# Loads held until the crossbar transposes of the batch ahead have landed, and a planner told shorter times for these, in an attention and gated-FFN kernel on one core

## The chip, the cores and the metric

The kernel runs on one core of a Trainium2 chip. The metric is the device time of one execution in microseconds (us). Medians of the kernel before lie between 450.0 and 451.1 us from one session to another; single executions lie between 448.9 and 453.2.

Engine names in the profile: PE is TensorE (matmuls), DVE is VectorE, ACT is ScalarE, POOL is GpSimd, SP is SyncE, and "SPq" marks SP's issuing of a DMA.

## The reference

```python
batch, n_heads, seq, head_dim = (8, 12, 448, 64)
scores = scale * q @ k.T                       # per batch and head
attn   = np.maximum(scores, 0.0) ** 2 / S
x      = (attn @ v) -> (B*S, H*D) = (3584, 768)
out    = (np.maximum(x @ w_gate, 0) * (x @ w_val)) @ w_out    # d_ff 1536
```

q, k and v come in float32 as (8, 12, 448, 64), the output is float32. The kernel computes in bfloat16.

## The kernel before

The eight batches run through attention and FFN. TensorE's program interleaves score products of one batch with FFN products of the batch before it, so that TensorE has FFN work while DVE and ACT work on the scores. A score product needs q and k with the head dimension on the partitions, so both have to be transposed. For batches 0 and 1 TensorE does this; for batches 2 to 7 it is done as follows:

1. GpSimd loads k and q of one batch into a tile qk (672 KB each as they land; there are two such tiles), and v into vv. All loads are issued from GpSimd's one in-order queue.
2. DVE copies qk in seven pieces into the tile `spare`, of which there is one.
3. SP issues two DMA transposes through the crossbar, q's half and k's half, from `spare` into qkT. SP also issues the stores of the output, in program order.

```python
def transpose_batch(b):
    ...
    def emit_pair(s, t):                       # step 2, seven DVE copies
        if s == 0:
            box["p"] = spare()[...]
        nc.vector.tensor_copy(box["p"][:, :, s], st.qk[:, :, t, :]...)
    ...
    def emit_x(i):                             # step 3
        nc.sync.dma_start_transpose(out=columns_of(b)[:, i]..., in_=box["p"][64 * i:64 * i + 64]...)
    xo = []
    for i in range(2):
        op = Op({"SP": 0.3}, lambda i=i: emit_x(i), deps=perm + xo[:1], alloc=[st.tbuf] if i == 0 else [],
                reads=[pair], xfer=9.0 if b > 2 else 6.0)
...
for b in range(2, B):                          # GpSimd's order of loads
    load_heads(b, 0, H, "k")                   # k and q
    if b > 3:
        load_heads(b - 1, 0, H, "v")
    if b == 2:
        load_heads(b, 0, H, "v")
    if b >= XBAR_FROM:
        transpose_batch(b)
```

The order of instructions on each engine is decided at build time by a small planner. It walks through all operations with a cost for each (`{"SP": 0.3}` is 0.3 us of SP, `xfer` the time of a transfer) and always starts what can start first. Its numbers never reach the chip. They only set the order of instructions; what waits for what is then settled by semaphores. For SP the end of an operation is its start plus its cost plus 2.0 plus `xfer`. The planner of the kernel before thus takes 0.3 + 2.0 + 6.0 us for a transpose of batch 2, and the second begins after the first (`xo[:1]`).

## Time and profile before

| | before |
|---|---|
| median of 3 runs | 450.43 us (449.41 to 451.0) |
| span of the profiled run | 449.1 us |
| TensorE busy | 428.7 us, 95% |
| TensorE's wait for qkT | 9.9 us, once |

The busy picture of the page has the span in 40 slices of 11.2 us. A digit is the busy share in tenths; PEclk is the clock granted to TensorE, in tenths of full speed; GB/s is what the DMA engines moved.

```profile
PE   6799999937999999999999999999999999999996
PEclk8899999996999999999999999999999999999999
DMA  8999999992693990579146800872002300030014
GB/s 111 198 198 199 202 205 221 197 200 33 80 201 83 166 165 13 93 115 199 18 61 106 168 1 2 123 122 55 1 0 71 74 0 1 1 83 23 1 35 105
```

TensorE is full from the third slice on, except in the ninth and tenth (90 to 112 us), and in the tenth its clock is low too. The DMA engines are full up to that hole, at about 200 GB/s. The list of TensorE's waits names the cause (columns: who waited for whom, us in total, times, longest):

```profile
PE s_ps L468 <- DMA qkT<-spare: 9.9, 1, 9.9
```

The timeline around the hole, in lines of SP, POOL and TensorE (columns: start, us, engine, line, operation, and in brackets the idle time before it with what ended it):

```profile
62.59 0.75 POOL L246 DMA_DIRECT2D qk<-in_k_dram  x1 [5.92 <-PE t_ps L346]
...
75.14 0.75 POOL L246 DMA_DIRECT2D qk<-in_k_dram  x1 [11.06 <-DVE spare L377]
...
75.84 11.20 SPq L387 DMA_TRANSPOSE qkT<-spare  x1
...
81.69 1.49 POOL L246 DMA_DIRECT2D vv<-in_v_dram  x2 [5.07 <-PE s_ps L530]
...
88.53 12.00 SPq L387 DMA_TRANSPOSE qkT<-spare  x1
...
104.22 1.30 PE L468 MATMUL s_ps<-qkT 64*128 64x448 bf16 x6 [9.94 <-DMA qkT<-spare]
...
105.46 2.42 PE L577 MATMUL v_ps<-xT,wv_102 128*128 128x448 bf16 x6
```

The two transposes of batch 2 take 11.2 and 12.0 us to be issued and land 20.9 and 15.6 us after their issue began, while the loads of q and k of batches 3 and 4 and of v of batch 3 run. TensorE stops until they have landed. The windows view shows that the hole costs again after its end (columns: window, length, busy us of PE, PEld, DVE, ACT, POOL, then granted clock, DMA share, GB/s):

```profile
94.30:104.20 9.90, 0.00 (x0) 0.00 (x0) 0.00 (x0) 0.54 (x1) 0.00 (x0) 0.76 1.20 179
104.20:110.00 5.80, 5.78 (x19) 2.17 (x20) 4.30 (x7) 1.35 (x2) 0.00 (x0) 0.52 0.00 0
110.00:112.00 2.00, 2.00 (x15) 0.77 (x13) 0.75 (x2) 1.07 (x3) 0.00 (x0) 1.00 0.00 0
```

For 5.8 us after the hole the granted clock is 0.52, and a product of six matmuls takes 2.42 instead of 1.30 us.

### The profile page before, as it was taken

Reading aid. Unit: us, or ns where it says so; the run is one execution under the profiler, and the core shown is the slowest. Engines: PE = TensorE matmul, PEld = TensorE weight load, DVE = VectorE, ACT = ScalarE, POOL = GpSimd, SP = SyncE. Lnnn points to the kernel's source line nnn. Section 1 sums busy time; section 2 is a strip of 40 time slices with the busy share of each in tenths; the row PEclk is TensorE's granted clock in tenths of the full one; section 3 lists DMA queues with packets and bytes.
Section 4 is the critical chain, followed back from the end, with each engine's and each line's share of the span. In section 5 each row is a group of like instructions: output and inputs, shape, how many; then the busy total and the mean of one; then the engine's idle time right before and its main releaser. Section 6 shows DMA issues by size and latency. Waiting matters only on the chain.

```text
span 449.1 us, 7413 instructions
## 1 busy us (share of the span) xinstructions
PE 428.7 (95%) x3014; PEld 224.7 (50%) x3014; DVE 232.2 (52%) x412; ACT 198.1 (44%) x339; POOL 45.3 (10%) x67
## 2 busy tenths in 40 slices
PE   6799999937999999999999999999999999999996
PEld 2477875412454444544445444454445444555553
DVE  2797875114865775666563467446554355402210
ACT  2685454212454545553453445553554443432221
POOL 8545211100100200020000100010000000000000
PEclk8899999996999999999999999999999999999999
DMA  8999999992693990579146800872002300030014
GB/s 111 198 198 199 202 205 221 197 200 33 80 201 83 166 165 13 93 115 199 18 61 106 168 1 2 123 122 55 1 0 71 74 0 1 1 83 23 1 35 105
DMA packets 75170, 44.12 MB, mean 98 GB/s; under 512 B 34560, under 2 KB 71680, under 8 KB 75136
## 3 DMA queue, kind: packets, MB, share of 16 engines
q0 software_dynamic: 37856, 24.38, 38.4%
q1 hardware_dynamic: 37200, 19.17, 22.8%
q8 instruction: 23, 0.38, 0.3%
q14 instruction: 11, 0.09, 0.1%
q10 hardware_dynamic: 80, 0.10, 0.1%
HBM read 48.76 MB, written 11.01 MB: 133 GB/s over the span
## 4 chain that ended last, share of the span: by engine, by line
PE 92%; DMA 4%; DVE 1%; ACT 1%; issue 1%; SPq 0%; POOL 0%; ACTq 0%; POOLq 0%
PE o_ps L629 25%; PE v_ps L577 24%; PE g_ps L577 24%; PE s_ps L468 7%; PE s_ps L530 6%; DMA qkT<-spare 3%; PE s_ps L474 2%; PE t_ps L346 1%; PE s_ps L524 1%; DMA qk<-in_q_dram 1%; PE x_ps L530 1%; DVE qkT L355 0%; ACT r_sb L484 0%; PE w_ps L334 0%; POOL qk L246 0%
## 5 line engine op out<-in xcount | busy, mean ns | idle before, releaser
L484 ACT ACTIVATE r_sb<-s_ps 128x896 bf16<-128x896 f32 (+4 forms) x145 | 99.5, 740 | 46.6 <-PE s_ps L468 35.5
L591 DVE TENSOR_TENSOR hT<-v_ps,g_sb 128x448 bf16<-128x448 f32 (+2 forms) x108 | 61.5, 569 | 105.9 <-PE v_ps L577 105.6
L502 DVE TENSOR_TENSOR at<-r_sb 128x896 bf16<-128x896 bf16 (+4 forms) x163 | 93.4, 611 | 21.3 <-ACT r_sb L484 20.9
L584 ACT ACTIVATE g_sb<-g_ps 128x448 bf16<-128x448 f32 (+2 forms) x106 | 53.8, 507 | 113.0 <-PE g_ps L577 110.2
L629 PEld LDWEIGHTS <-hT 128*128 128x128 bf16 x672 | 63.9, 98 | 48.9 <-issue 8.4
L486 DVE TENSOR_SCALAR r_sb<-s_ps 128x896 bf16<-128x896 f32 (+5 forms) x73 | 63.2, 894 | 46.7 <-PE s_ps L468 46.3
L629 PE MATMUL o_ps<-wo_106,hT 128*128 128x384 bf16 x336 | 59.4, 327 | 0.0
L629 PE MATMUL o_ps<-wo_107,hT 128*128 128x384 bf16 x336 | 59.2, 326 | 0.0
L642 ACT ACTIVATE o_sb<-o_ps 128x384 f32<-128x384 f32 (+1 forms) x56 | 27.3, 487 | 72.4 <-PE o_ps L629 72.4
L468 PE MATMUL s_ps<-qkT 64*128 64x448 bf16 (+2 forms) x324 | 38.1, 340 | 12.9 <-DMA qkT<-spare 9.9
L246 POOL DMA_DIRECT2D vv<-in_v_dram x22 | 15.4, 708 | 187.0 <-PE s_ps L530 177.3
L468 PEld LDWEIGHTS <-qkT 64*128 64x128 bf16 x324 | 11.7, 95 | 34.1 <-issue 16.1
L530 PE MATMUL s_ps<-at,vv 128*64 128x448 bf16 x252 | 27.8, 357 | 0.0
L546 ACT CAST xT<-s_ps 128x896 bf16<-128x896 f32 (+1 forms) x22 | 19.6, 891 | 12.8 <-PE s_ps L530 12.8
L530 PEld LDWEIGHTS <-vv 128*64 128x64 bf16 x324 | 15.6, 109 | 14.0 <-issue 7.0
L577 PE MATMUL v_ps<-xT,wv_102 128*128 128x448 bf16 (+2 forms) x108 | 22.3, 344 | 0.0
L577 PE MATMUL g_ps<-xT,wg_97 128*128 128x448 bf16 (+2 forms) x108 | 22.2, 344 | 0.0
L577 PE MATMUL g_ps<-xT,wg_94 128*128 128x448 bf16 (+2 forms) x108 | 21.4, 332 | 0.1
L577 PE MATMUL g_ps<-xT,wg_96 128*128 128x448 bf16 (+2 forms) x108 | 21.2, 332 | 0.0
L577 PE MATMUL g_ps<-xT,wg_99 128*128 128x448 bf16 (+2 forms) x108 | 21.2, 332 | 0.0
L577 PE MATMUL g_ps<-xT,wg_98 128*128 128x448 bf16 (+2 forms) x108 | 21.2, 332 | 0.0
L577 PE MATMUL g_ps<-xT,wg_95 128*128 128x448 bf16 (+2 forms) x108 | 21.2, 332 | 0.0
(62 smaller groups left out, 339.0 us busy)
## 6 DMA issues: line engine op xcount, KB each, us to landing
out_dram<-o_sb SPq DMA_DIRECT2D x54, 192.0 KB, 2.7
vv<-in_v_dram POOLq DMA_DIRECT2D x12, 384.0 KB, 10.5
qk<-in_k_dram POOLq DMA_DIRECT2D x6, 672.0 KB, 16.3
qk<-in_q_dram POOLq DMA_DIRECT2D x6, 672.0 KB, 20.0
wo_106<-in_moe_w_out_dram POOLq DMA_DIRECT2D x1, 1152.0 KB, 15.7
wo_107<-in_moe_w_out_dram POOLq DMA_DIRECT2D x1, 1152.0 KB, 19.4
qk<-in_k_dram POOLq DMA_DIRECT2D x5, 224.0 KB, 10.6
qk<-in_q_dram POOLq DMA_DIRECT2D x5, 224.0 KB, 9.1
```

What stands on the lines that cost most here:

```text
L246: op = Op({"POOL": 0.58 + 0.0004 * n_desc}, lambda: nc.gpsimd.dma_start(out=dst(), in_=src), deps=deps, alloc=alloc, xfer=kb / rate)
L468: nc.tensor.matmul(half_of(h2)[:, m * n:(m + 1) * n], lhsT=kq(1, j, h2, key_off(b) + c * 128, 128), rhs=kq(0, j, h2, self.c0, n), start=Tr ...
L484: nc.scalar.activation(dst, src, AF.Relu)
L486: nc.vector.tensor_scalar_max(dst, src, 0.0)
L502: lambda: nc.vector.tensor_tensor(self.at_tile(i), loc["r"][:, :2 * ne], loc["r"][:, :2 * ne], ALU.mult),
L530: nc.tensor.matmul(x_of(o, j), lhsT=st.vv[:, 4 * g + 2 * j + h2, 1 + c, :], rhs=self.at(j, c, h2), start=False, stop=(c == NC - 1))
L546: nc.scalar.copy(dst, src)
L577: nc.tensor.matmul(ps, lhsT=w[c][:, kd, o:o + 128], rhs=st.xT[:, kd, cols], start=(kd == 0), stop=(kd == KD - 1))
L584: nc.scalar.activation(loc["gs"], loc["g_ps"], AF.Relu)
L591: nc.vector.tensor_tensor(hs["hT"][:, mf, t0:t0 + n], loc["v_ps"], loc["gs"], ALU.mult)
L629: nc.tensor.matmul(loc["o"], lhsT=hs["hT"][:, kf, ti * 128:(ti + 1) * 128], rhs=w_out_sb[hf][:, kf, :], start=(kf == 0), stop=(kf == KF - 1))
L642: nc.scalar.activation(out=dst, in_=src, func=AF.Copy, scale=float(out_scale))
```

## The change

The intent: no load of q and k for the next batch shall run beside the transposes of the batch ahead. GpSimd copies one element per partition out of the last transposed tile ("the gate"). The copy has to wait until the transposes have landed, and everything behind it in GpSimd's queue waits with it, v included. The planner's numbers are set to what a transpose was expected to need alone, and the two transposes may follow each other directly.

```diff
-            op = Op({"SP": 0.3}, lambda i=i: emit_x(i), deps=perm + xo[:1], alloc=[st.tbuf] if i == 0 else [],
-                    reads=[pair], xfer=9.0 if b > 2 else 6.0)
+            op = Op({"SP": 4.5}, lambda i=i: emit_x(i), deps=perm, alloc=[st.tbuf] if i == 0 else [],
+                    reads=[pair], xfer=1.0)
...
+        return xo
...
+    mark = const.tile([P2, 1], BF16)
+
+    def gate(b, done):
+        pool_ops.append(Op({"POOL": 0.1}, lambda: nc.gpsimd.tensor_copy(mark, columns_of(b)[:P2, 1, HP - 1, S - 1:]),
+                           deps=done))
+
     for b in range(2, B):
+        if b > 2:
+            gate(b - 1, done)
         load_heads(b, 0, H, "k")
         if b > 3:
             load_heads(b - 1, 0, H, "v")
         if b == 2:
             load_heads(b, 0, H, "v")
-        if b >= XBAR_FROM:
-            transpose_batch(b)
+        done = transpose_batch(b)
```

Compared instruction by instruction, the built programs differ in order. At batch 2, the transposes now stand in a pair before two stores, and the first score product of batch 2 stands four products of six matmuls earlier on TensorE.

## The prediction

> **What bounds the kernel now.** TensorE: busy 428.7 of 449.1 us (the page's first part), 92% of the chain that ended last. After the start-up there is one hole: in the list of waits TensorE waits 9.9 us, once, for the crossbar transpose that makes qkT, and for nothing else after 60 us. The timeline puts it at 94.3 to 104.2 us, before the first score product of batch 2. It costs twice: the windows view gives a granted clock of 0.52 from 104.2 to 110.0 us, so 5.8 x 0.48 = 2.8 us more are lost. Together 12.7 us, 2.8% of the time.
>
> **Why the wait is there.** The DVE copies for batch 2 end at 75 us and the first transpose is issued at 75.84. It took 11.2 us to issue and 20.9 to land; the second was issued at 88.53 (after two stores) and landed after 15.6, at 104.2. Later pairs, alone (280.3 and 284.3 us), take 4.0 us of issue each and land after 7.0 and 7.8. From 60 to 104 us the DMA engines moved 180 to 220 GB/s, mostly loads: k, q of batch 3 (issued 62.6, landed 85.5), of batch 4 (75.1, landed 95.4), v of batch 3 (81.7, landed 102.6). The Trainium skill, "DMA: Bandwidth & Descriptors", section "Issuing engines are not separate DMA queues", says that DMAs of all issuers interleave on the same 16 engines; this trace agrees, 20.9 us against 7.0.
>
> **What the change does.** A one-element copy on GpSimd reads the last transposed tile, so all later loads in that in-order queue wait for both transposes of the batch before. Added: five such copies, on an engine with time. The planner's new costs (4.5 us of SP for a transpose, no chain between the two) put the two transposes back to back before the two stores, and move batch 2's first score product four products of six matmuls (4.6 us) earlier: wanted at about 89.4 instead of 94.2 us. TensorE's total work is unchanged.
>
> **Sum.** The copies still end near 75 us (q of batch 2 landed at 71.4, ahead of the removed traffic). Transposes are issued at 75.8 and 79.9 and land near 83 and 87.8 (estimate: 75.84 + 4.0 + 7.8, from the late pair), 1 to 2 us before TensorE wants them: no wait, no clock loss. Loads of batch 3 start near 88 instead of 62.6 and land by about 98; its transposes run near 116 to 129, and batch 3 is wanted near 135 (147.8 now, less 12.7). v of batch 3 lands near 143, wanted near 151. No new wait, with 6 to 8 us of slack; later batches have more. Gain 12.7 us: predicted 437.8, range 435.5 to 441.5. Chances: faster by over 2% 0.86, within 2% 0.13, slower 0.01.
>
> **What would show it right.** The wait for qkT below 1 us; granted clock 1.00 from 20 us on; each transpose landing after 7 to 9 us, the first pair before 89 us; loads of batch 3 issued right after; span shorter by hole plus slow stretch. **Wrong:** a rest of the wait at 89 us, a wait before batch 3 near 130 us because loads, copies and transposes now run one after the other, or SP held by two transposes in a row, so that stores free o_sb late.
>
> **What would make me wrong.** There are only 1 to 2 us of slack at batch 2; a wait of a few us would also bring back part of the clock loss. Or transposes are slow in this stretch by themselves, not by the loads.

## The result, and the profile after

The changed kernel takes 438.24 us (median of 4 runs, 437.95 to 439.76), the kernel before 450.02 us in the same comparison (4 runs, 449.41 to 451.0). The ratio is 0.9743, with a 95% interval of 0.9713 to 0.9773: 2.6% faster. Ratios in this document are the mean time of one kernel's fast runs over that of the other's of the same rounds, so not quite the ratio of the medians.

The busy picture after:

```profile
PE   6799999999999999999999999999999999999996
PEclk9689999999999999999999999999999999999999
DMA  7999999982189647918956990990002200040014
GB/s 104 192 198 198 202 202 188 143 138 46 17 145 199 110 69 101 228 37 126 143 91 105 167 162 3 135 171 1 1 1 76 71 0 2 4 105 0 1 36 108
```

The hole is gone from the PE row, and PEclk is full from the fourth slice on. In the eighth and ninth slices (77 to 99 us) the DMA engines now move 143 and 138 GB/s in place of 197 and 200, and the loads come in separate stretches later. TensorE's one wait for qkT:

```profile
PE s_ps L469 <- DMA qkT<-spare: 0.2, 1, 0.2
```

The timeline where the hole was:

```profile
77.34 9.87 SPq L387 DMA_TRANSPOSE qkT<-spare  x2
...
89.95 1.30 PE L578 MATMUL g_ps<-xT,wg_95 128*128 128x448 bf16 x6
...
91.40 0.74 PE L469 MATMUL s_ps<-qkT 64*128 64x448 bf16 x6 [0.15 <-DMA qkT<-spare]
91.41 0.18 POOL L712 COPY mark<-qkT 64x1 bf16<-64x1 bf16 x1 [33.31 <-DMA qkT<-spare]
...
91.89 0.75 POOL L246 DMA_DIRECT2D qk<-in_k_dram  x1 [0.31 <-PE s_ps L469]
```

The pair is issued in 9.9 us in all and lands after 7.6 and 9.4 us; the score product follows with almost no wait, the gate opens in the same moment, and only then do the loads of batch 3 go out (62.6 us before). The product after the score product takes 1.31 us, so the clock did not fall:

```profile
89.00:94.30 5.30, 5.15 (x30) 2.38 (x29) 3.10 (x5) 2.41 (x4) 1.67 (x3) 1.00 0.48 92
94.30:104.20 9.90, 9.90 (x58) 4.66 (x56) 7.35 (x13) 4.33 (x7) 0.00 (x0) 1.00 0.83 134
```

Where the time went: the hole (9.9 less 0.2 us) and the slow stretch (about 2.8 us) make 12.5 us. The two profiled spans differ by 11.0 us, but in this profile of the changed kernel everything stood 1.5 us later already before the transposes (its first transpose is issued at 77.34 against 75.84 us), from its start-up: from 20 to 24 us its granted clock was 0.50, where the kernel before had 1.00. 11.0 + 1.5 is 12.5. A second profile of the changed kernel (number 12) has a clock of 1.00 there, so this is not due to the change.

### The profile page after: what moved, and what is told of

Same layout as the page of the kernel before. It is cut to its first block, busy times and chain, and to the rows that moved or that the text cites. A ratio compares the mean times of both kernels' runs of the same rounds, so it can differ in the third digit from the quotient of the medians.

```text
span 438.1 us, 7425 instructions
## 1 busy us (share of the span) xinstructions
PE 427.1 (98%) x3014; PEld 224.9 (51%) x3014; DVE 231.6 (53%) x411; ACT 199.2 (45%) x340; POOL 46.2 (11%) x72
## 4 chain that ended last, share of the span: by engine, by line
PE 93%; DMA 4%; POOL 1%; issue 0%; DVE 0%; SPq 0%; ACT 0%; POOLq 0%
PE o_ps L630 25%; PE g_ps L578 25%; PE v_ps L578 25%; PE s_ps L469 7%; PE s_ps L531 6%; DMA qkT<-spare 2%; DMA qk<-in_q_dram 2%; PE s_ps L475 2%; PE x_ps L531 1%; PE s_ps L525 1%; POOL qk L246 1%; PE t_ps L346 1%; PE x_ps L525 0%; POOL vv L246 0%; DVE qkT L355 0%
## 5 line engine op out<-in xcount | busy, mean ns | idle before, releaser
L503 DVE TENSOR_TENSOR at<-r_sb 128x896 bf16<-128x896 bf16 (+4 forms) x163 | 93.6, 612 | 22.8 <-ACT r_sb L485 22.6
L487 DVE TENSOR_SCALAR r_sb<-s_ps 128x448 bf16<-128x448 f32 (+5 forms) x72 | 62.5, 898 | 50.7 <-PE s_ps L469 50.5
L547 ACT CAST xT<-s_ps 128x896 bf16<-128x896 f32 (+1 forms) x22 | 19.6, 891 | 12.7 <-PE s_ps L531 12.7
L531 PEld LDWEIGHTS <-vv 128*64 128x64 bf16 x324 | 16.7, 115 | 14.5 <-issue 7.7
L469 PEld LDWEIGHTS <-qkT 64*128 64x128 bf16 x324 | 11.8, 96 | 22.4 <-issue 15.6
L578 PE MATMUL g_ps<-xT,wg_96 128*128 128x448 bf16 (+2 forms) x108 | 21.2, 332 | 0.0
L578 PE MATMUL g_ps<-xT,wg_99 128*128 128x448 bf16 (+2 forms) x108 | 21.2, 332 | 0.0
L578 PE MATMUL g_ps<-xT,wg_97 128*128 128x448 bf16 (+2 forms) x108 | 21.2, 332 | 0.0
L578 PE MATMUL v_ps<-xT,wv_102 128*128 128x448 bf16 (+2 forms) x108 | 21.2, 332 | 0.0
L578 PE MATMUL v_ps<-xT,wv_101 128*128 128x448 bf16 (+2 forms) x108 | 21.2, 332 | 0.0
L578 PE MATMUL g_ps<-xT,wg_98 128*128 128x448 bf16 (+2 forms) x108 | 21.2, 332 | 0.0
L578 PE MATMUL g_ps<-xT,wg_95 128*128 128x448 bf16 (+2 forms) x108 | 21.2, 332 | 0.0
## 6 DMA issues: line engine op xcount, KB each, us to landing
wo_107<-in_moe_w_out_dram POOLq DMA_DIRECT2D x1, 1152.0 KB, 20.3
```

Source lines behind the costliest of these rows:

```text
L469: nc.tensor.matmul(half_of(h2)[:, m * n:(m + 1) * n], lhsT=kq(1, j, h2, key_off(b) + c * 128, 128), rhs=kq(0, j, h2, self.c0, n), start=Tr ...
L487: nc.vector.tensor_scalar_max(dst, src, 0.0)
L503: lambda: nc.vector.tensor_tensor(self.at_tile(i), loc["r"][:, :2 * ne], loc["r"][:, :2 * ne], ALU.mult),
L531: nc.tensor.matmul(x_of(o, j), lhsT=st.vv[:, 4 * g + 2 * j + h2, 1 + c, :], rhs=self.at(j, c, h2), start=False, stop=(c == NC - 1))
L547: nc.scalar.copy(dst, src)
L578: nc.tensor.matmul(ps, lhsT=w[c][:, kd, o:o + 128], rhs=st.xT[:, kd, cols], start=(kd == 0), stop=(kd == KD - 1))
```

## The experiments

The prediction was met, but that does not show that its reasons are right: the change has two halves, the gates and the planner's new numbers, and either might have done it. **Contention theory**: the transposes of batch 2 are late because loads run beside them; the gate is what helps. **Order theory** (the rival): the second transpose was late because it stood behind stores on SP, and TensorE's order was unlucky; the new order is what helps. A third question is what the four later gates do, as the kernel before waits nowhere but at batch 2. Each kernel gave the right result. The edits shown are against the full change, except in numbers 5 and 11, which start from the kernel before. "Idle" below is TensorE's idle time from 60 to 420 us in the windows view, 10.1 us in the kernel before and 0.3 in the changed one.

### 1. The planner's new numbers without gates

```diff
-        if b > 2:
-            gate(b - 1, done)
```

> The planner's new costs alone, no gate: the two transposes stand back to back on SP before the stores and the first score product of batch 2 stands 4 products earlier, but the loads run as before. Contention theory (the loads slow the transposes): each transpose still takes over 14 us to land, the second lands near 102 us, TensorE wants it at about 89.5 and waits 11 to 13 us; 450 to 453 us, no gain or a little slower. Order theory (what gained was the order of the transposes on SP and of the products on TensorE): the pair lands before 90 us, wait below 1 us, about 438 us.

Measured: 467.09 us (ratio 1.0365, 1.0335 to 1.0394). At batch 2 the contention theory is right: the transposes land after 21.3 and 16.4 us and TensorE waits 13.8 us:

```profile
PE s_ps L469 <- DMA qkT<-spare: 13.8, 1, 13.8
```

The pair stood before the stores and was slow all the same, so the order theory is out. But the time was expected at no more than 453 us, and idle is 22.8 us. The other 9 us come in the following batches, from DVE. DVE's list of waits, from 60 to 300 us, has a large entry, and the timeline shows what it does to TensorE:

```profile
DVE spare L377 <- DMA qkT<-spare: 47.2, 5, 16.5
```

```profile
159.08 1.30 PE L578 MATMUL g_ps<-xT,wg 128*128 128x448 bf16 x6
163.30 0.36 DVE L377 COPY spare<-qk 128x768 bf16<-128x768 bf16 x1 [16.45 <-DMA qkT<-spare]
...
164.24 1.55 PE L469 MATMUL s_ps<-qkT 64*128 64x448 bf16 x6 [3.87 <-DVE r_sb L487]
```

The copy into `spare` for the next batch waits 16.45 us for the transposes that still read `spare`, and everything behind it in DVE's in-order program waits with it; then TensorE waits for DVE. The planner, told that a transpose is over soon, had put this copy early.

### 2. The gates with the planner's old numbers

```diff
-            op = Op({"SP": 4.5}, lambda i=i: emit_x(i), deps=perm, ...
-                    reads=[pair], xfer=1.0)
+            op = Op({"SP": 0.3}, lambda i=i: emit_x(i), deps=perm + xo[:1], ...
+                    reads=[pair], xfer=9.0 if b > 2 else 6.0)
```

> The gate alone with the planner's old costs: two stores stand between the two transposes again and the first score product of batch 2 is wanted at about 94 us. Contention theory: transposes land after 7 to 9 us each, the second near 91 to 92 us, no wait, 438 us (437 to 440). Order theory: the wait of some 10 us stays, about 450 us.

Measured: 448.80 us (0.9971, 0.9943 to 0.9998), idle 7.5 us. At batch 2 the gate did all that was expected of it: the pair had landed at 91.6 us, and TensorE did not wait. But the gain was lost at batch 4, in lines of SP and TensorE:

```profile
169.52 4.16 SPq L387 DMA_TRANSPOSE qkT<-spare  x1
175.87 6.87 SPq L674 DMA_DIRECT2D out_dram<-o_sb  x4
182.78 4.67 SPq L387 DMA_TRANSPOSE qkT<-spare  x1
...
189.86 1.68 PE L469 MATMUL s_ps<-qkT 64*128 64x448 bf16 x8 [4.88 <-DMA qkT<-spare]
```

With gates, transposes, loads, copies and the next transposes form a chain from batch to batch. In the old order two or four stores, which wait for their own data, stand between the two transposes and stretch the chain: the second transpose of batch 4 is begun 13.3 us after the first, where in the full change it is 4.6 us at batch 2, and every pair is issued in 9.3 to 9.9 us. (That batch 4 also begins late here has another reason, see number 8.) Both theories named a time, 438 or 450 us, and neither gave this reason for 449.

### 3. Only the first gate

```diff
-        if b > 2:
+        if b == 3:
             gate(b - 1, done)
```

> Planner's new costs, but only the first of the five gates (loads of batch 3 held until batch 2 is transposed). If only batch 2's transposes were on the critical path: within 0.3% of the full change (437.5 to 439.5 us), even though later transposes again land after 11 us and more beside loads. Rival (every gate gives a part): slower than the full change by 1 us or more per gate left out.

Measured: 445.63 us (0.9895, 0.9869 to 0.9920), idle 5.5 us. My expectation fails. The loads of batch 5 run beside the transposes of batch 3, and TensorE waits there:

```profile
115.67 16.51 SPq L387 DMA_TRANSPOSE qkT<-spare  x2
...
136.95 0.74 PE L469 MATMUL s_ps<-qkT 64*128 64x448 bf16 x6 [2.38 <-DMA qkT<-spare]
```

In the kernel before, the transposes of batch 3 landed nearly as late (134.5 against 136.9 us), but were wanted only at 147.8 us. Without the hole, batch 3 is wanted 13 us sooner (TensorE begins to wait at 134.6), and the slack that hid its contention is gone. This wait is 2.4 of the 5.5 us of idle. The other 3.0 us are waits of TensorE for ACT (1.3) and DVE (1.1 and 0.6); DVE waited 23.4 us for `spare`, as in number 1. The later gates are part of the gain.

### 4. A gate that opens after the first transpose of each pair

```diff
-            gate(b - 1, done)
+            gate(b - 1, done[:1])           # and the copy reads half 0 of qkT instead of half 1
```

> As the full change, but every gate waits for the first transpose of the pair alone, so that the loads of batch 3 start near 85 us and run beside the second transpose. Contention theory: first transpose still lands after 7 to 8 us, the second later than 9.4 us, 10 to 14 us after its issue; TensorE waits 1 to 4 us at batch 2; 439 to 443 us. Order theory: no change, 438.2 us.

Measured: 442.17 us (0.9820, 0.9788 to 0.9851), idle 3.7 us, as expected. The first transpose lands after 7.4 us; the second, beside the loads that start at 83.4 us, after 12.8; TensorE waits 3.5 us at batch 2 and for no later transpose. The landings of the two transposes (the first, their median, the second) and the wait:

```profile
DMA to landing us min/median/max: 7.4/10.1/12.8
...
92.95 0.79 PE L469 MATMUL s_ps<-qkT 64*128 64x448 bf16 x6 [3.52 <-DMA qkT<-spare]
```

### 5. No gate, the planner told that batch 2 takes longer

```diff
-                    reads=[pair], xfer=9.0 if b > 2 else 6.0)
+                    reads=[pair], xfer=9.0 if b > 2 else 11.0)
```

> The kernel before with one number changed: the planner is told 11 instead of 6 us for a transpose of batch 2, so it puts the first score product of batch 2 later on TensorE (near 105 us) and other products ahead of it; no gate, loads as before. If the gain of the change is only the hole that TensorE had: the transposes still take 15 us and more and land near 104 us, but the wait is below 2 us and the granted clock stays 1.00; 437.5 to 440 us. Rival (holding the loads gains something besides the hole): it stays 3 us or more above the full change.

Measured: 439.81 us (0.9774, 0.9741 to 0.9807), idle 1.7 us. This is the kernel before with one number changed. The transposes are as slow as ever (11.1 us of issue for the first), but TensorE has other products in front of the score product:

```profile
105.07 0.74 PE L468 MATMUL s_ps<-qkT 64*128 64x448 bf16 x6 [0.70 <-DMA qkT<-spare]
```

So nearly the whole gain is the hole: covering the wait is worth almost as much as removing its cause. The 95% intervals of this run and of the full change overlap, so the 1.6 us between them are not clear of noise, though the idle time (1.7 against 0.3 us) points the same way.

### 6. The first gate behind the loads of q and k of batch 3

```diff
-        if b > 2:
+        if b > 3:
             gate(b - 1, done)
         load_heads(b, 0, H, "k")
+        if b == 3:
+            gate(b - 1, done)
```

> As the full change, but the first gate stands behind the loads of q and k of batch 3: they go out at about 63 us as before, and only q, k of batch 4 and v of batch 3 are held. Contention theory: a part of the traffic is back, the pair lands at 92 to 95 us, TensorE (which wants it at 89.5) waits 3 to 6 us and the clock falls for a while; 441 to 446 us. Order theory: 438.2 us.

Measured: 441.52 us (0.9799, 0.9768 to 0.9830), idle 2.6 us. Now it is the first transpose that runs beside loads and lands after 12.7 us, while the second lands after 7.3, at 93.7 us; the wait at batch 2 is 2.4 us, a little below the 3 to 6 us expected, and the clock, which was expected to fall, did not. The landings of the first and the second transpose, and the wait:

```profile
DMA to landing us min/median/max: 12.7/12.7/12.7
DMA to landing us min/median/max: 7.3/7.3/7.3
...
93.79 0.74 PE L469 MATMUL s_ps<-qkT 64*128 64x448 bf16 x6 [2.44 <-DMA qkT<-spare]
```

This with number 4 ties the slow transpose to the overlap: in number 4 the second of the pair is slow, here the first, each time the one that the loads meet. The windows just after the wait, of number 4 and then of this one:

```profile
92.90:94.90 2.00, 1.95 (x10) 0.77 (x11) 1.52 (x2) 1.35 (x2) 0.00 (x0) 0.65 1.22 245
94.90:97.00 2.10, 2.10 (x8) 0.78 (x7) 1.51 (x4) 0.00 (x0) 0.00 (x0) 0.52 1.10 178
```

```profile
93.80:96.00 2.20, 2.20 (x15) 1.00 (x16) 2.14 (x4) 1.35 (x2) 0.18 (x1) 1.00 0.57 151
```

After 3.5 us of idling the clock fell, after 2.4 us it did not. The Trainium skill, "TensorE: Matmul & The Clock Gate", section "What's actually happening", gives an idle window of about 3.4 us as what turns the clock down to half; these two runs fit that, and so does the hole before (9.9 us, then 0.52). They do not show that 3.4 us is a safe limit. In short windows of the profiles the clock fell 5.2 us after TensorE had stopped in the kernel before, 4.1 us after in number 4, but 2.6 us after in number 2 and 2.0 us after in number 10; and in number 3 it fell after waits of 2.4 and 1.3 us with 0.7 us of work between. Number 6 may have been spared by luck.

### 7. The pair together on SP, no gate

```diff
-        if b > 2:
-            gate(b - 1, done)
...
-                    reads=[pair], xfer=1.0)
+                    reads=[pair], xfer=8.0)
```

> No gate; two transposes back to back on SP before the two stores, first score product of batch 2 at about 96.5 us (planner told 8 us of transfer). Separates the order on SP from the place on TensorE. Contention theory: each transpose takes 14 us and more, the second lands at 100 to 103 us, wait 4 to 7 us and a clock loss of about 2.5; 445 to 449 us. Order theory (the second transpose was late because it stood behind the stores): lands before 90, no wait, 438 us.

Measured: 446.82 us (0.9919, 0.9889 to 0.9948), idle 7.5 us. Both transposes stand before the stores and are as slow as in the kernel before, landing after 21.2 and 16.8 us; TensorE waits 7.3 us, and afterwards the clock is 0.50 for 4 us:

```profile
PE s_ps L469 <- DMA qkT<-spare: 7.3, 1, 7.3
```

The order on SP without the gate does not make a transpose faster. This run differs from number 1 in one number, 8 instead of 1 us of `xfer`, and is 20 us faster: DVE's wait for `spare` is 8.2 us in place of 47.2, and TensorE waits nowhere after batch 2.

### 8. All gates, pair together, the planner told 8 us

```diff
-                    reads=[pair], xfer=1.0)
+                    reads=[pair], xfer=8.0)
```

> All five gates, pairs back to back on SP as in the full change, but the planner is told 8 us of transfer instead of 1, so TensorE wants batch 2 some two products later than in the kernel before (near 96 us). The gate alone lost its gain in batch 4, whose second transpose stood 13 us behind the first because stores lay between them on SP. If that split is what spoilt it: no wait for qkT over 1 us at any batch, 437.5 to 440 us. If instead the gate needs the early places on TensorE: 444 us or more, with waits at batch 3 or 4.

Measured: 442.74 us (0.9826, 0.9793 to 0.9859), idle 3.3 us, between the two expectations. There is no wait for qkT at any batch, so the split of the pair was what made number 2 wait for it. What remains is another cost of being late:

```profile
184.07 0.99 PE L469 MATMUL s_ps<-qkT 64*128 64x448 bf16 x8
185.81 0.37 PE L469 MATMUL s_ps<-qkT 64*128 64x448 bf16 x2 [0.75 <-DVE r_sb L487]
...
187.89 0.38 PE L475 MATMUL s_ps<-qkT 64*64 64x448 bf16 x4 [1.12 <-ACT r_sb L485]
```

Batch 4 starts so late that score products follow one another without FFN products between them (the first pair of batch 4 is issued at 168.4 us, in the full change at 157.4), and TensorE waits for DVE and ACT, which evict the scores. In number 2 this first transpose was issued just as late (169.5 us), so the split explains number 2's wait, not the late start. Nor are the loads the reason: in this run k and q of batch 4 had landed by 151.0 us, but the last copies into `spare` end at 168.2 (157.3 in the full change), because they stand later in DVE's program. What the two runs share is a planner that was told a longer time. The idle time accounts for 3.0 of the 4.5 us by which the medians differ; the profile of this run also shows 2.3 us of waiting for a weight load in the first 60 us, which has nothing to do with the change. I leave the rest open.

### 9. The first two gates only

```diff
-        if b > 2:
+        if b in (3, 4):
             gate(b - 1, done)
```

> The full change with only the first two gates (batches 3 and 4). With one gate, batch 3 was late by 2.4 us because its transposes ran beside the loads of batch 5 and the removed hole had eaten the slack. Theory (each batch that has lost its slack needs its gate, later ones have more slack): wait at batch 3 gone, 438 to 441 us. Rival (the planner's optimistic costs are wrong wherever a gate is missing, and DVE is held by copies that wait for the one spare buffer): waits of DVE for spare and of TensorE for DVE appear at batches 4 to 6, 442 us or more.

Measured: 449.85 us (0.9985, 0.9932 to 1.0038): the whole gain is lost, though only three of the five gates were taken out, all of them for batches far from the hole. It is 4.2 us slower than number 3, which keeps only one gate where this run keeps two, so the loss is no sum over gates. The wait at batch 3 is gone as my theory had it, but the time is the rival's. In the timeline:

```profile
156.03 20.23 SPq L387 DMA_TRANSPOSE qkT<-spare  x2
...
178.54 0.36 DVE L377 COPY spare<-qk 128x768 bf16<-128x768 bf16 x1 [8.94 <-DMA qkT<-spare]
179.49 4.21 PE L630 MATMUL o_ps<-wo,hT 128*128 128x384 bf16 x13 [6.17 <-DVE hT L592]
```

The first batch without a gate behind it has its pair issued in 20.2 us; DVE, whose copy stands where the planner thought the pair was done, waits 8.9 us for `spare`, and TensorE waits 6.2 us for what DVE would have done behind that copy, then runs at a clock of 0.50 for over 3 us.

### 10. Two gates, the other batches told to the planner as slower

```diff
-        if b > 2:
+        if b in (3, 4):
             gate(b - 1, done)
...
-                    reads=[pair], xfer=1.0)
+                    reads=[pair], xfer=1.0 if b < 4 else 10.0)
```

> Two gates (batches 3 and 4) as in the run that lost the whole gain, but for the batches whose transposes now run beside loads (4 to 7) the planner is told 10 us of transfer instead of 1. Theory: what lost the gain was that the planner, told that a transpose lands early, put DVE's copies for the next batch too early in DVE's in-order queue, where they wait for the one spare buffer and hold the work behind them. Then DVE's wait for spare falls from 19.7 to below 6 us, TensorE's waits from 8.3 to below 2, and the time is 438.5 to 441 us. Rival (the loads themselves, running beside the later transposes, cost the time): it stays at 447 to 450 us.

Measured: 443.98 us (0.9843, 0.9802 to 0.9883), between the two expectations. DVE's wait for `spare` fell from 19.7 to 14.1 us only, TensorE's waits from 8.3 to 5.5. So the planner's number explains about a half of what number 9 lost. In batches 4 and 5 each transpose took 16.8 to 20.3 us to land, against the 16.5 us (4.5 + 2.0 + 10.0) that the planner was told, so it was still told too little; whether the right number would recover all was not tried.

### 11. No gate, 12 us told instead of 11

```diff
-                    reads=[pair], xfer=9.0 if b > 2 else 6.0)
+                    reads=[pair], xfer=9.0 if b > 2 else 12.0)
```

> As the kernel before with the planner told 12 instead of 11 us for a transpose of batch 2 (no gate). The 0.7 us that was left of the wait at batch 2 should be gone; 438.5 to 440 us, the same as with 11 or up to 1 us less; level with the full change within 0.5%.

Measured: 439.78 us (0.9748, 0.9712 to 0.9783), as with 11. The wait for qkT is gone, idle is 1.1 us. Beside number 12, from the same session, the two intervals overlap: these runs do not tell the two kernels apart.

### 12. The full change again

No edit.

> The full change again, beside the runs of this call: 438.2 us (437.5 to 439.8), wait for qkT at batch 2 below 1 us; no later wait.

Measured: 438.20 us (0.9725, 0.9691 to 0.9760) beside numbers 8, 9 and 11. No wait for qkT at all.

### All runs side by side

| kernel | median us | idle of TensorE, 60 to 420 us |
|---|---|---|
| before | 450.0 to 451.1 | 10.1 |
| full change (two sessions) | 438.24, 438.20 | 0.3, 0.1 |
| 1 numbers, no gates | 467.09 | 22.8 |
| 2 gates, old numbers | 448.80 | 7.5 |
| 3 first gate only | 445.63 | 5.5 |
| 4 gates on the first half | 442.17 | 3.7 |
| 5, 11 no gate, told 11 or 12 us | 439.81, 439.78 | 1.7, 1.1 |
| 6 gate behind batch 3's loads | 441.52 | 2.6 |
| 7 pair together, no gate | 446.82 | 7.5 |
| 8 all gates, told 8 us | 442.74 | 3.3 |
| 9 first two gates | 449.85 | 8.4 |
| 10 first two gates, told 10 us | 443.98 | 5.7 |

The times follow the idle time: a kernel is slower than the full change by its extra idle time, with up to a half more on top (twice in number 11, where both are about 1 us), part of it the slow clock after idle stretches of several us. No run was faster than the full change; with 0.1 to 0.3 us of idle left after 60 us there is little to win in this part of the kernel.

## Why the prediction was right

- **The bound and the hole.** Predicted: a hole of 9.9 us plus 2.8 us of slow clock, 12.7 us in all, and nothing else on the path. The medians differ by 11.8 us (450.02 less 438.24), the profiles by 11.0, or 12.5 after the start-up is set off. The predicted time was 437.8, the measured 438.24 us.
- **The cause at batch 2.** Predicted: loads beside the transposes. Runs 1 and 7 have the new order without the gate and transposes of 16.4 to 21.3 us; the full change and run 2 have the gate and none of it; runs 4 and 6 move the overlap from one transpose to the other and the slowness moves along. The cited sentence of the Trainium skill, that DMAs of all issuers interleave on the same engines, fits all of them. What exactly transposes and loads share was not tested; the runs show only that a transpose is slow where loads run beside it.
- **The margin at batch 2.** Predicted: landing 1 to 2 us before TensorE wants the pair. Measured: 0.15 us after, as the second transpose was issued 4.6 and not 4.0 us behind the first, and took 9.4 and not 7.8 us. ("4.0 us of issue each" misreads the late pair: it was 4.0 and 5.3 us.) So this term of the sum was too small by 2 us and the whole margin was used up. The prediction named it as its weak point; that it cost only 0.2 us is in part luck, as number 4 shows: there a wait of 3.5 us at this place cost 3.9.
- **The clock.** Predicted: 1.00 from 20 us on. Measured: 1.00 around batch 2 and later, but 0.50 from 20 to 24 us in the first profile of the changed kernel; number 12 had 1.00 there.
- **Batch 3.** Predicted: transposes from 116 to 129 us, wanted near 135. Measured: issued at 118.0, landed by 131.6 (the gate opens), wanted at 136.8: 5.2 us of slack against 6 predicted. v of batch 3 landed later than predicted (148.8 against 143 us) and still caused no wait.
- **What it did not say.** The prediction treated the planner's numbers as a side effect and the gates of batches 4 to 7 as harmless. The runs show that they carry the result: the numbers without gates cost 16 us (run 1), the gates with the old numbers gain next to nothing (run 2), and leaving out gates where the kernel before never waited costs 7 to 12 us (runs 3 and 9). Its sentence "later batches have more" holds in the full change (7.3 us of slack at batch 4, 13.9 at batch 5), where transposes take 6.9 to 9.4 us and the planner is told about that; with gates missing it does not.

## What to carry to other kernels

Before removing the cause of a wait, look whether the program merely comes too early for what it waits for: one number that told the planner how long the transposes really take (run 5) gave nearly the whole gain without any gate. Where an order is planned with assumed latencies and the engines run it strictly in order, the assumption and the hardware must change together, and in every batch; a too-short latency puts an instruction early that then holds all that stands behind it. And removing a hole makes everything after it due earlier, so transfers that were late behind the hole without harm have to be looked at again.

## What the Trainium skill lacked or had wrong

- "DMA: Bandwidth & Descriptors", section "Rules for kernel authors", says of a transpose next to ordinary DMAs that it needs nothing. No wrong result was seen here, so this holds for correctness, but the cost is missing: landing in 6.9 to 9.4 us where loads are kept away and in up to 21.3 us beside them.
- The same page, section "Issuing engines are not separate DMA queues", calls the sequencer's time to start a DMA usually small. For a crossbar transpose of 672 KB it is not: 4.0 to 5.5 us of SP where no loads run, more than half of the 7 to 9 us to landing, and up to 14.5 us beside loads (number 10; 11.2 to 12.6 us at batch 2 without a gate), during which the stores behind it on SP wait.
- "Advanced Engine Details and Errata", section "X-Bar Transpose (TRN2)", says that transposes are as fast as regular DMAs, and expects 350 to 400 GB/s. From issue to landing, one transpose alone is about as fast as one load (7.0 us for 672 KB, against 6.4 us for the load of k of batch 3 in the profile after, which lands as many bytes but reads float32). The rate was not reached: 688128 bytes in 7.0 us are 98 GB/s, and while the last pair of the kernel before ran without loads (280 to 290 us) the DMA engines moved 121 GB/s; from 22 to 60 us, with mostly loads, they moved 200.
